# A scan on TensorE whose outputs leave transposed, and the place of its visits between two layers of a gated feed-forward network

## The chip, the core and the metric

The kernel runs on one core of one Trainium2 chip. The metric is the device time of one execution in microseconds (us); the median of three runs is compared. TensorE is called PE below, VectorE DVE, ScalarE ACT, GpSimd POOL and SyncE SP, as in the profile.

## The reference

Two layers, one behind the other. The first is a linear recurrence over 768 steps for 4 sequences of 8 heads with 48 lanes each; its outputs, 3072 rows of 384, go through a gated feed-forward network with 1536 hidden lanes.

```python
state = np.zeros((B, H, D, D))                      # B=4, H=8, D=48
for t in range(S):                                  # S=768
    cur = einsum('bhd,bhe->bhde', u[None] * kt, vt)
    y[:, :, t] = einsum('bhd,bhde->bhe', rt, state + cur)
    state = wt[:, :, :, None] * state + einsum('bhd,bhe->bhde', kt, vt)
...
gate = 1 / (1 + exp(-(x @ w_gate)))                 # x: 3072 x 384, w_gate: 384 x 1536
val = x @ w_val
out = (gate * val) @ w_out
```

## The kernel before

The scan is cut into 24 chunks `q`, each 128 steps of one sequence: `q % 4` is the sequence, `q // 4` the stretch of time. Four chunks of one stretch make a block of 512 rows for the network, `n = q // 4`, so there are six blocks.

For one chunk the two decay scans, `prep_k` (L328) and `prep_r` (L347), run on DVE and scale k and r in place in the tile `pin`; `fade` (L341) scales the old state. PE turns the scaled k (`turn_k`, L361, the tile `pk`) and ACT copies it out. `section1` makes the scores and the sums for the new state (`scores` L374, `sums` L388, the pair of banks `pa`). DVE masks the scores and adds up two states (`settle`). Then the outputs are made (`states` L402 from the stored states, `mix` L417 from masked scores and values, the tile `py`). Here 128 steps lie on the partitions: the scan's outputs have to be turned before the network can use them. So ACT copies them to SBUF (`take_y`, L469), PE turns them (`turn_x`, L472, the tile `px`), ACT takes the rounded part and DVE the remainder (`take_x`, `rest_x`). POOL makes the diagonal (`bonus1` to `bonus4`).

The network works on one of twelve slices `f` of 128 hidden lanes at a time: nine matmuls of `gate` (`pg`, L510), nine of `value` (`pu`, L510), and nine of `down` (`po`, L550), each 128x128 by 512 rows. DVE multiplies gate and value (L528), ACT rounds the product (`hidden_hi`, L532), DVE takes the remainder (`hidden_lo`, L536).

The program is in two stages. In the **first stage** block 0 of the network runs together with chunks 0 to 7 and with the unpacking of the twelve weight slices; a list scheduler (`Plan`) with written costs and ranks (`TURNS`, `COMES`, `LAGS`, `LATE`) fixes the order in which instructions are issued on each engine. In the **main loop** blocks 1 to 5 run in 60 steps `(n, f)`; chunks 8 to 23 are put between. Each step has four slots, and the order on PE is

```python
slot(0); gate(*a); sigmoid(*a)
slot(1); value(*a); hidden(*a); hidden_hi(*a); hidden_lo(*a)
slot(2); down(f - 1)
slot(3)
```

A chunk's outputs and the next chunk's `section1` are issued together, in `both(q)`, which is called the **visit** of q. Slot numbers run on (4 to a step), and what prepares chunk q+1 is put at fixed distances ahead of the visit of q: `prep_k` and `fade` 7 slots before, `turn_k` 5 before, `prep_r` 3 before. A visit stands at slot 7 + 12j of a block in the steady part, that is in slot 3 of a step, behind `down` and ahead of the next `gate`; `FIRST` has the four places of block 1. Engines take their instructions in the order of issue, and wait where an operand is not there. SP issues the loads of later chunks (`load`), and an empty instruction on it (`relay`) hands a bank from one half of PE's rows to the other.

## Time and profile before

| | before |
|---|---|
| median of 3 runs | 586.2 us (586.17 to 589.35) |
| the profiled execution | 585.72 us |
| its span | 583.6 us, granted PE clock 0.996 |
| PE busy | 550.7 us (94%) |
| DVE busy | 325.8 us (56%) |
| ACT busy | 204.6 us (35%) |
| POOL busy | 106.1 us (18%) |

The span reaches from the first to the last instruction of the profiled execution; 2.1 us of its time lie around it. All times within the trace are counted from the start of the span.

### The profile page before, as it was taken

Reading aid. Unit: us, or ns where it says so; the run is one execution under the profiler, and the core shown is the slowest. Engines: PE = TensorE matmul, PEld = TensorE weight load, DVE = VectorE, ACT = ScalarE, POOL = GpSimd, SP = SyncE. Lnnn points to the kernel's source line nnn. Section 1 sums busy time; section 2 is a strip of 40 time slices with the busy share of each in tenths; the row PEclk is TensorE's granted clock in tenths of the full one; section 3 lists DMA queues with packets and bytes.
Section 4 is the critical chain, followed back from the end, with each engine's and each line's share of the span. In section 5 each row is a group of like instructions: output and inputs, shape, how many; then the busy total and the mean of one; then the engine's idle time right before and its main releaser. Section 6 shows DMA issues by size and latency. Waiting matters only on the chain.

```text
span 583.6 us, 13560 instructions
## 1 busy us (share of the span) xinstructions
PE 550.7 (94%) x6044; PEld 460.0 (79%) x6044; DVE 325.8 (56%) x461; ACT 204.6 (35%) x384; POOL 106.1 (18%) x89
## 2 busy tenths in 40 slices
PE   3589999999998999999999999999999999999994
PEld 2468889998777888788888788888788888788883
DVE  4999999976765644554654654654644621221221
ACT  2756596443332323423323323323423322321121
POOL 4540522130211320220210220210220200000000
PEclk9999999999999999999999999999999999999998
DMA  8763925341320222232132231132231100100001
GB/s 269 240 249 91 400 95 171 124 123 50 109 90 11 80 89 56 90 90 57 34 90 55 89 90 54 38 89 59 86 90 47 44 1 2 54 2 0 1 0 60
DMA packets 11046, 50.60 MB, mean 87 GB/s; under 512 B 1265, under 2 KB 1266, under 8 KB 9442
## 3 DMA queue, kind: packets, MB, share of 16 engines
q1 hardware_dynamic: 8818, 45.70, 24.5%
q10 hardware_dynamic: 2160, 3.93, 1.8%
q8 instruction: 49, 0.80, 0.6%
q14 instruction: 19, 0.16, 0.1%
HBM read 44.91 MB, written 4.72 MB: 85 GB/s over the span
## 4 chain that ended last, share of the span: by engine, by line
PE 89%; DVE 5%; DMA 2%; issue 2%; ACT 1%; SPq 0%; DVEq 0%
PE pg L510 24%; PE pu L510 23%; PE po L550 21%; PE py L425 3%; PE py L412 3%; PE pg L507 3%; PE pu L507 3%; PE po L546 3%; PE pa L383 2%; DMA pin<-dec 2%; PE pk L364 2%; PE pa L396 2%; PE px L475 1%; DVE sg L528 1%; DVE hl L536 1%
## 5 line engine op out<-in xcount | busy, mean ns | idle before, releaser
L510 PE MATMUL pg<-x,w 128*128 128x512 f32 (+1 forms) x648 | 153.2, 379 | 0.4 <-ACT sg L521 0.2
L510 PE MATMUL pu<-x,w 128*128 128x512 f32 (+1 forms) x648 | 148.2, 373 | 0.3 <-DVE sg L528 0.3
L528 DVE TENSOR_TENSOR sg<-pu,sg 128x512 f32<-128x512 f32 (+1 forms) x84 | 51.5, 613 | 167.8 <-PE pu L510 162.3
L510 PEld LDWEIGHTS pu<-x,w 128*128 128x128 f32 x648 | 115.2, 188 | 21.9 <-DVE sg L528 0.5
L510 PEld LDWEIGHTS pg<-x,w 128*128 128x128 f32 x648 | 113.3, 188 | 24.2 <-DVE x L495 2.2
L550 PE MATMUL po<-hh,w 128*128 128x512 f32 (+1 forms) x432 | 128.8, 382 | 0.0
L532 ACT CAST hh<-sg 128x512 fp32r<-128x512 f32 (+1 forms) x72 | 42.1, 584 | 129.3 <-DVE sg L528 129.3
L550 PEld LDWEIGHTS po<-hh,w 128*128 128x128 f32 x432 | 77.1, 188 | 12.7
L521 ACT ACTIVATE sg<-pg 128x512 f32<-128x512 f32 (+1 forms) x84 | 44.8, 533 | 111.4 <-PE pg L510 105.4
L550 PE MATMUL po<-hl,w 128*128 128x512 f32 (+1 forms) x216 | 80.6, 373 | 0.7 <-DVE hl L536 0.7
L313 POOL TENSOR_TENSOR bon<-tok,ub 128x384 f32<-128x384 f32 x24 | 34.2, 1424 | 227.7 <-DMA tok<-tok 169.9
L536 DVE TENSOR_TENSOR hl<-sg,hh 128x512 fp32r<-128x512 f32 (+1 forms) x72 | 48.9, 679 | 41.8 <-ACT hh L532 41.7
L326 POOL TENSOR_TENSOR at<-eye,a 128x512 f32<-128x512 f32 x24 | 29.0, 1212 | 129.0 <-DVE a L320 106.1
L550 PEld LDWEIGHTS po<-hl,w 128*128 128x128 f32 x216 | 40.6, 188 | 8.7 <-DVE hl L536 1.2
L316 POOL TENSOR_TENSOR bon<-bon,tok 128x384 f32<-128x384 f32 x24 | 40.1, 1670 | 1.9
L333 DVE TENSOR_TENSOR_SCAN eg<-pin,ends 112x516 f32<-112x516 f32 x24 | 35.4, 1477 | 6.4 <-DMA pin<-dec 5.7
L359 ACT ACTIVATE eg<-eg 112x1032 f32<-112x1032 f32 x24 | 25.6, 1067 | 33.6 <-DVE pin L355 31.7
L412 PE MATMUL py<-mid,pin 48*64 48x48 f32 x384 | 27.0, 228 | 4.4 <-DVE at L452 4.4
L350 DVE TENSOR_TENSOR_SCAN eg<-pin,heads 112x516 f32<-112x516 f32 x24 | 29.9, 1245 | 0.0
L470 ACT COPY bon<-py 128x384 f32<-128x384 f32 x24 | 11.5, 479 | 52.1 <-PE py L425 52.1
L452 DVE COPY_PREDICATED at<-after,pa 128x512 f32<-128x512 int32 x24 | 17.5, 730 | 19.4 <-PE py L412 15.1
L412 PEld LDWEIGHTS py<-mid,pin 48*64 48x64 f32 x384 | 22.4, 140 | 5.4 <-ACT sq L260 4.8
(72 smaller groups left out, 579.6 us busy)
## 6 DMA issues: line engine op xcount, KB each, us to landing
pin<-dec SPq DMA_DIRECT2D x23, 675.5 KB, 5.8
tok<-tok SPq DMA_DIRECT2D x24, 576.0 KB, 6.1
raw<-wts SPq DMA_DIRECT2D x12, 1152.0 KB, 12.1
y<-o ACTq DMA_DIRECT2D x15, 256.0 KB, 2.0
y<-o SPq DMA_DIRECT2D x3, 256.0 KB, 3.3
pin<-dec SPq DMA_DIRECT2D x1, 448.0 KB, 3.9
pin<-dec SPq DMA_DIRECT2D x1, 227.5 KB, 2.8
line<-u SPq DMA_DIRECT2D x1, 1.5 KB
```

The source lines that it names most:

```text
L313: nc.gpsimd.tensor_tensor(out=bon[q], in0=tk[q][:, 0:DM], in1=ub, op=ALU.mult)
L316: nc.gpsimd.tensor_tensor(out=bon[q], in0=bon[q], in1=tk[q][:, DM:2 * DM], op=ALU.mult)
L333: nc.vector.tensor_tensor_scan(out=e[:, 516:0:-1], data0=t[:, 516:0:-1], data1=ends[:, 516:0:-1], initial=0.0, op0=ALU.mult, op1=ALU.add,)
L350: nc.vector.tensor_tensor_scan(out=e[:, WW:WW + 516], data0=t[:, 0:516], data1=heads[:, 0:516], initial=0.0, op0=ALU.mult, op1=ALU.add,)
L412: todo[o].append(lambda p=p, s=s, half=half, o=o, sl=sl: nc.tensor.matmul(spots[o][half, p], lhsT=rr(q)[sl, p, half], rhs=(mid if s else r ...
L507: nc.tensor.matmul(t, lhsT=full(f)[:, cols], rhs=whole[n][:, k, spot], start=k == 0, stop=k == NKT - 1)
L510: nc.tensor.matmul(t, lhsT=w[f][:, cols], rhs=x[n][:, a, k, spot], start=k == 0 and j == 0, stop=k == NKT - 1 and j == 2)
L521: nc.scalar.activation(sg, hid["g", n, f, i0], AF.Sigmoid)
L528: nc.vector.tensor_tensor(out=sg, in0=hid["u", n, f, i0], in1=sg, op=ALU.mult)
L532: nc.scalar.copy(hh, hid["s", n, f, i0])
L536: nc.vector.tensor_tensor(out=hl, in0=hid["s", n, f, i0], in1=hid["hi", n, f, i0].bitcast(F32), op=ALU.subtract)
L550: nc.tensor.matmul(to, lhsT=w[f][:, cols], rhs=h, start=first and i == 0, stop=last and i == 2, skip_group_check=True)
```

## The change

1. In the visit, values and states become the stationary operand, in pieces of 32 lanes, and scores and r become the moving one, 64 steps wide. The outputs then leave with the lanes on the partitions, so `take_y` and `turn_x` go. `scores` and `sums` are cut into stationary pieces of 32 lanes too, so that all matmuls of a visit are in 64x32 tiles.
2. The 48 lanes of a head don't fill whole tiles. Two thirds of the 384 output rows are final; the last third comes in two halves, one in each bank, that have to be added. ACT copies one half (`take_x`), DVE adds the other (`join_x`), ACT rounds it (`last_x`), DVE takes the remainders (`low_x`, `low_last`). The rows of the two upward weights are put in the matching order on the host; values and states get padded places (`tok` grows from 1152 to 1216 columns, the states stand 64 apart in `wide`).
3. The outputs of a visit stand in the bank `turn` and in the bank `pu` that `value` uses. So a visit moves to slot 1, between `gate` and `value`, and at such a step the pending `down` is issued right behind the visit, ahead of `value`.
4. The written costs, ranks and orders of the first stage are new.

```diff
-TURNS = "c0 c1 c2 w0 w1 w2 c3 w3 w4 w5 w6 w7 c4 w8 w9 c5 c6 w10 c7 w11"
+TURNS = "c0 w0 c1 c2 w1 w2 w3 c3 w4 w5 w6 w7 w8 w9 c4 w10 w11 c5 c6 c7"
...
-LAGS = [0, -3.0]
+LAGS = [0, 4.0]
...
-FIRST = [11, 21, 32, 43]
+FIRST = [13, 25, 33, 45]
...
     def scores(q):
...
+                for i in range(half.start, half.stop, 32):
+                    for o in range(2):
+                        sl = slice(64 * o, 64 * o + D)
+                        nc.tensor.matmul(
+                            t[i:i + 32, o, p * HC:(p + 1) * HC], lhsT=kk(q)[sl, p, i:i + 32], rhs=rr(q)[sl, p, half], start=True, stop=True,
+                            skip_group_check=True)
...
+    def states(q):
+        for j in range(2):
             for s, half in enumerate(HALVES):
                 if q < B and not s:
                     continue
+                for p in range(NP):
+                    for o in range(2):
+                        sl = slice(64 * o, 64 * o + D)
+                        i = 64 * p + ((16, 48), (32, 0))[o][j]
+                        nc.tensor.matmul(
+                            lhsT=(mid if s else ready)[q][sl, i:i + 32], rhs=rr(q)[sl, p, half], stop=False, **placed(q, o, p, j, half))
+
+    def mix(q, turn):
+        done = []
+        for j in range(2):
             for p in range(NP):
+                for s, half in enumerate(HALVES):
+                    o = s ^ turn
+                    i = VO + p * L + ((0, 32), (80, 48))[o][j]
+                    done.append(nc.tensor.matmul(
+                        lhsT=tk[q][half, i:i + 32], rhs=att[q][half, o, p], stop=True, **placed(q, o, p, j, half)).ins)
+        return done
...
-    def take_y(q):
-        nc.scalar.copy(bon[q].rearrange("a (p o e) -> a o p e", o=2, e=D), bank["yy", q])
-
-    def turn_x(q):
...
     def both(q):
...
+        bank["y", q] = [att_bank(f"py{q}"), ps1.tile([P, 512], F32, tag="pu", name=f"pz{q}")]
+        states(q)
+        step = relay(mix(q, 0))
+        if q + 1 < NG:
+            section1(q + 1)
+        follow(step, mix(q, 1))
+        take_x(q)
+        join_x(q)
+        last_x(q)
+        low_x(q)
+        low_last(q)
...
-    visit = {q: (q - start) // B * row + (7 + 12 * (q % B) if q >= start + B else FIRST[q - start]) for q in range(start, NG)}
+    visit = {q: (q - start) // B * row + (9 + 12 * (q % B) if q >= start + B else FIRST[q - start]) for q in range(start, NG)}
...
+            visits = ((n - R0) * NFF + f) * 4 + 1 in visit.values()
             slot(1)
+            if visits:
+                down(*last.pop())
             value(*a)
```

How the instructions stand now. In the rows the first number of `pg`, `pu`, `po`, `sg`, `hl` names a group or bank and the second is the slice f; numbers behind the last underscore tell tiles apart.

**PE in block 3, steps 5 to 7, before:** the matmuls around `turn_k` (`pk`) of the next chunk.

```order
L550 MATMUL po_2_3791<-hl_0_4_4020,w_723 128x512
L510 MATMUL pg_0_6_4174<-x_2997,w_1076 128x512 x9
L510 MATMUL pu_0_6_4186<-x_2997,w_1076 128x512 x9
L364 MATMUL pk_4201<-ident,pin_4119 128x112 x4
L550 MATMUL po_0_3789<-hh_0_5_4146,w_869 128x512 x2
L550 MATMUL po_0_3789<-hl_0_5_4148,w_869 128x512
```

**The same place with the change:**

```order
L545 MATMUL pg_0_6_5017<-x_3581,w_1283 128x512 x9
L545 MATMUL pu_0_6_5029<-x_3581,w_1283 128x512 x9
L585 MATMUL po_0_4544<-hh_0_5_5013,w_1041 128x512 x2
L585 MATMUL po_0_4544<-hl_0_5_5015,w_1041 128x512
L585 MATMUL po_1_4545<-hh_0_5_5013,w_1041 128x512 x2
L585 MATMUL po_1_4545<-hl_0_5_5015,w_1041 128x512
L585 MATMUL po_2_4546<-hh_0_5_5013,w_1041 128x512 x2
L585 MATMUL po_2_4546<-hl_0_5_5015,w_1041 128x512
L373 MATMUL pk_5061<-ident,pin_4989 128x112 x4
L545 MATMUL pg_0_7_5068<-x_3581,w_1356 128x512 x9
```

`turn_k` stood behind `value` and ahead of `down`; it now stands behind both, ahead of the next `gate`.

**DVE at the same place, before:** `prep_k` (the scan into `eg`, the reciprocal, the product into `pin`), `fade`, and the products of the network around them.

```order
L528 TENSOR_TENSOR sg_0_5_4133<-pu_0_5_4135,sg_0_5_4133 128x512
L536 TENSOR_TENSOR hl_0_5_4148<-sg_0_5_4133,hh_0_5_4146 128x512
L495 TENSOR_TENSOR x_3924<-px_4150,x_3924 128x3x128
L333 SCALAR_TENSOR_TENSOR eg_4168<-pin_4119,ends 112x516
L337 RECIPROCAL heads<-eg_4168 112x4
L339 TENSOR_TENSOR pin_4119<-pin_4119,eg_4168 112x512
L345 TENSOR_TENSOR ready_4172<-state_104,eg_4168 112x192
L528 TENSOR_TENSOR sg_0_6_4184<-pu_0_6_4186,sg_0_6_4184 128x512
```

**With the change:**

```order
L571 TENSOR_TENSOR hl_0_5_5015<-sg_0_5_4844,hh_0_5_5013 128x512
L563 TENSOR_TENSOR sg_0_6_5027<-pu_0_6_5029,sg_0_6_5027 128x512
L571 TENSOR_TENSOR hl_0_6_5042<-sg_0_6_5027,hh_0_6_5040 128x512
L339 SCALAR_TENSOR_TENSOR eg_5047<-pin_4989,ends 112x516
L343 RECIPROCAL heads<-eg_5047 112x4
L345 TENSOR_TENSOR pin_4989<-pin_4989,eg_5047 112x512
L354 TENSOR_TENSOR wide_105<-state_103,eg_5047 112x4x48
L563 TENSOR_TENSOR sg_0_7_5078<-pu_0_7_5080,sg_0_7_5078 128x512
```

The scan stood ahead of the two products of step 6; it now stands behind both of them.

**PE in block 1 with the change, step 6,** where the visit of chunk 9 has taken its `down` with it and chunk 11 is prepared (before, a `down` stood between `value` and this `pk`):

```order
L585 MATMUL po_2_2294<-hl_0_5_2614,w_1041 128x512
L545 MATMUL pu_0_6_2800<-x_1298,w_1283 128x512 x9
L373 MATMUL pk_2823<-ident,pin_2787 128x112 x4
L545 MATMUL pg_0_7_2830<-x_1298,w_1356 128x512 x9
L545 MATMUL pu_0_7_2842<-x_1298,w_1356 128x512 x9
```

`turn_k` stands right behind `value` there, with no matmul between.

## The prediction

> **What bounds the kernel now.** First the page: totals, then busy tenths in 40 slices of 14.6 us (9 is 90% or more). Then a table by stretches: length, busy time of PE, weight loads, DVE, ACT, POOL, granted clock, DMA share.

> ```profile
> span 583.6 us, 13560 instructions
> ...
> PE   3589999999998999999999999999999999999994
> ...
> DVE  4999999976765644554654654654644621221221
> ...
> 60.00:90.00 30.00, 28.88 (x344) 26.79 (x343) 29.27 (x40) 20.85 (x39) 11.45 (x6) 1.00 0.56 231
> 145.90:208.37 62.47, 58.96 (x774) 48.04 (x773) 38.29 (x58) 19.64 (x37) 13.98 (x10) 1.00 0.22 68
> 208.37:295.90 87.53, 87.48 (x993) 71.90 (x993) 45.86 (x70) 26.17 (x51) 15.76 (x12) 1.00 0.23 69
> ```

> The first stage (to 146 us) fills DVE and PE alike: 29.27 and 28.88 of 30 us. In the main loop PE has 87.48 of 87.53 us and DVE half: whatever PE does or waits for there counts in full, and DVE counts only where PE waits for it. The chain of waits shows one cycle of three steps (start, us, what):

> ```profile
> 274.10 2.28 PE pg L510 x9
> 276.38 2.06 PE pu L510 x9
> 278.43 0.33 PE px L475 x3
> 278.76 2.09 PE po L550 x9
> ...
> 291.52 2.04 PE po L550 x9
> ```

> Nine matmuls take 2.04 us undisturbed; the transposes `px` take 0.33 and lengthen what follows by 0.05. The visit itself, in order of time (start, us):

> ```profile
> 293.17 0.39 PE L550 MATMUL po<-hl,w 128*128 128x512 f32 x1
> 293.49 0.25 PE L412 MATMUL py<-ready,pin 48*64 48x48 f32 x1
> ...
> 293.58 0.22 PE L412 MATMUL py<-ready,pin 48*64 48x48 f32 x1
> ...
> 293.64 0.22 PE L412 MATMUL py<-ready,pin 48*64 48x48 f32 x1
> ...
> 295.02 0.88 PE L425 MATMUL py<-tok,at 64*32 64x48 f32 x64
> 295.83 0.96 PE L510 MATMUL pg<-x,w 128*128 128x512 f32 x3
> ```

> It lasts from 293.49 to 295.83, 2.34 us. A tile of PE starts a new matmul every 0.06 us in the 64x64 part (293.58, 293.64); in the 64x32 part 64 of them start within 0.88 - 0.2 = 0.68 us on four tiles, 0.042 us each.

> **Part 1, the transposes go.** 16 visits in the main loop x (0.33 + 0.05) = **-6.1 us**. ACT's copy `take_y` lies beside matmuls and gives nothing.

> **Part 2, the visit in 64x32 tiles.** Each fp32 matmul is recorded twice. Now there are 4 x 32 matmuls, 256 records, evenly over eight tiles: 32 on each, 24 with 64 moving columns and 8 with 48. At 0.058 us and 0.042 us that is 24 x 0.058 + 8 x 0.042 = 1.73 us, with 0.13 to leave the mode (0.81 us from 295.02 to 295.83, less 0.68) 1.86 us, **-0.5 us a visit, -8 for 16**. The trace shows only four tiles busy at a time, so eight is the unknown. Upper end: four at a time, 48 x 0.058 + 16 x 0.042 + 0.13 = 3.6 us, +1.25 a visit. Lower end: every record at 0.042, 1.5 us, -0.85. I take eight, because sharing is already the rule in the row: four 64x32 tiles each keep their own 0.042 us. [...]

> [...]

> **Part 3, the visit moves; what was behind and ahead of it.** `value` waits until the bank `pu` is read out, by a copy and two activations on ACT and a remainder on DVE. Groups (busy, mean ns):

> ```profile
> L495 DVE TENSOR_TENSOR x<-px,x 128x384 fp32r<-128x384 f32 x22 | 12.1, 552 | 4.9 <-ACT x L490 4.9
> L470 ACT COPY bon<-py 128x384 f32<-128x384 f32 x24 | 11.5, 479 | 52.1 <-PE py L425 52.1
> L467 DVE TENSOR_TENSOR state<-pa,mid 112x192 f32<-112x192 f32 x20 | 7.1, 353 | 0.4
> L490 ACT ACTIVATION_READ_ACCUMULATOR x<-px 128x1 f32 x22 | 4.2, 193 | 0.0
> ```

> At 128 columns a DVE operation is 353 - 64 x (552 - 353)/192 = 0.29 us, an ACT one below 0.35. Three on ACT, two reads of 0.19 and one on DVE make at most 1.7 us; the `down` now ahead of `value` is 2.04. Cover holds: **0**; were it gone, up to 1.7 a visit. The wider `tok` (1216 columns for 1152) lands 5% later, long before its visit: 0.

> But the fixed distances move too. `prep_k` was issued in slot 0 and `turn_k` in slot 2, with `gate` and `value` (4.1 us) between; now they fall in slot 2 of one step and slot 0 of the next, with one `down` (2.04 us) between, and on DVE the scan stands behind both products of the step, which wait for `value`. The trace of before has one such place: chunk 9's visit stood in slot 21, a slot 1, and its `turn_k` had the same neighbours.

> ```profile
> 169.63 2.22 PE L510 MATMUL pu<-x,w 128*128 128x512 f32 x9
> ...
> 171.96 0.69 DVE L528 TENSOR_TENSOR sg<-pu,sg 128x512 f32<-128x512 f32 x1 [2.35 <-PE pu L510]
> ...
> 172.68 0.62 ACT L532 CAST hh<-sg 128x512 fp32r<-128x512 f32 x1 [2.19 <-DVE sg L528]
> ...
> 173.34 0.69 DVE L536 TENSOR_TENSOR hl<-sg,hh 128x512 fp32r<-128x512 f32 x1 [0.69 <-ACT hh L532]
> ...
> 173.51 1.38 POOL L313 TENSOR_TENSOR bon<-tok,ub 128x384 f32<-128x384 f32 x1 [7.42 <-DMA tok<-tok]
> ...
> 173.88 0.39 PE L550 MATMUL po<-hl,w 128*128 128x512 f32 x1
> 173.94 0.55 DVE L495 TENSOR_TENSOR x<-px,x 128x384 fp32r<-128x384 f32 x1
> 174.41 1.56 DVE L333 TENSOR_TENSOR_SCAN eg<-pin,ends 112x516 f32<-112x516 f32 x1
> 174.96 1.80 POOL L316 TENSOR_TENSOR bon<-bon,tok 128x384 f32<-128x384 f32 x1
> 176.01 0.18 DVE L337 RECIPROCAL heads<-eg 112x4 f32<-112x4 f32 x1
> 176.10 1.21 DVE L339 TENSOR_TENSOR pin<-pin,eg 112x512 f32<-112x512 f32 x1
> ...
> 177.41 0.57 PE L364 MATMUL pk<-ident,pin 112*128 112x112 f32 x4 [3.15 <-issue]
> ```

> PE stands idle for 3.15 us: the scaled k that `pk` reads is finished at 177.31. That it is not so in the steady part of before, and how fast DVE is without POOL beside it, show the rows of the later cycle:

> ```profile
> 282.74 2.21 PE L510 MATMUL pu<-x,w 128*128 128x512 f32 x9
> ...
> 283.55 0.66 DVE L339 TENSOR_TENSOR pin<-pin,eg 112x512 f32<-112x512 f32 x1
> ...
> 284.79 0.55 PE L364 MATMUL pk<-ident,pin 112*128 112x112 f32 x4
> ...
> 287.05 1.23 DVE L350 TENSOR_TENSOR_SCAN eg<-pin,heads 112x516 f32<-112x516 f32 x1
> ```

> There the product ends at 284.21, ahead of the end of `value`. With the change, from the start of L528 on: 2.07 us to the end of L536 (171.96 to 174.03), 1.23 for the scan, 0.13 to the product's start (176.10 less 174.41 less 1.56), 0.66, and 0.10 to `pk` (177.41 less 177.31): 4.19. L528 starts 0.11 after `value` ends (169.63 + 2.22 = 171.85), so PE has finished `down` at 2.04 - 0.11 = 1.93. **The stall is 4.19 - 1.93 = 2.26 us.** Behind `pk` on PE stands the next `gate`, and nothing passes it: the stall counts in full. The values without POOL hold if POOL is done:

> ```profile
> 167.62 0.35 SPq L300 DMA_DIRECT2D tok<-tok  x1
> ```

> POOL started (173.51) 5.9 us after this issue of its load, which follows a visit's end, and its two operations took 1.38 + 1.80 at the stall: done some 9 us after the visit, while the scan starts at 2.1 + 3 x 2.04 + 0.1 + 2.07 = 10.4. This happens for chunks 10 and 12 to 23: 13 x 2.26 = **+29.4**. With POOL beside it, each would be 2.07 + 1.56 + 0.13 + 1.21 + 0.10 - 1.93 = 3.14, the upper end.

> For chunk 11 the visit of chunk 9 has taken `down` away, and `pk` follows `value` at once; the scan starts 2.1 + 2.05 + 0.1 + 2.07 = 6.3 us after that visit, when POOL works: 5.07 + 0.11 = **+5.2**. The stall of 3.15 at chunk 10's `pk` in before is already within the 29.4: **-3.15**.

> **Part 4, the first stage.** Per chunk DVE gets 0.29 + 0.42 + 0.29 for 0.55 us (chunks 0 and 1: 0.29 for nothing): +3.3 in all; PE saves 8 x (0.38 + 0.3), at most 5.5. Both engines are nearly full and the order is new, so ends are -5 and +6; nearest to the DVE row: **+1**.

> **Sum**, against the profiled execution's 585.7 (median of the runs 586.2): -6.1 - 8 + 29.4 + 5.2 - 3.15 + 1 = +18.3: **604 us**.

> [...] Here 3.15 idle us left the clock at 1.00 in the stretch 145.90:208.37. [...]

> **The rivals.** (a) Only four tiles run at once: 16 x (1.25 + 0.5) = 28 more, **632**. For it: no row shows more than four; against: they didn't slow each other. (b) POOL is beside every scan: 13 x (3.14 - 2.26) = 11.4 more, **615**. For it: L339 took 1.21 at the stall; against: POOL's timing above. (c) The other side: `pk` doesn't wait, because DVE has the scan done within `down`. It decides at 1.93 us from L528's start; then 604 - 29.4 - 5.2 = **569.5**. For it: the steady cycle of before has no such stall; against: the scan stands behind products that alone take 2.07. (d) That `pk` is no longer at that place, or the tiles don't run as written: the issue order shows both, no weight.

> **How the numbers follow.** Forecast 0.63, (a) 0.14, (b) 0.15, (c) 0.08. The forecast's own spread: stalls between 1.9 and 2.6 (5 us either way), the first stage (5), the visit (0.35 x 16 = 6 below): 593 to 614. With (b) the range is 592 to 622, which leaves out most of (a) and (c). One per cent (5.9 us) is about what a measurement of this kernel tells from no change. Slower 0.90, same 0.04 (short stalls, fast visits), faster 0.06.

> **What would show it.** Right: idle before `pk` of 2.0 to 2.5 us 13 times, released by DVE's product, and one near 5; a block of 87.5 us becomes 87.5 + 4 x (2.26 - 0.88) = 93; no `px`; visits near 1.9 us; no idle before `pu`. Wrong: visits above 2.3 us (tiles), scans of 1.5 us (POOL), a main loop that starts more than 6 us from 146, or no idle before `pk`.

## The result, and the profile after

The changed kernel takes 674.7 us (median of four runs, 668.5 to 678.2) against 586.2 before: a ratio of 1.148, 95% interval 1.140 to 1.157. Slower was right; the forecast of 604, and its range to 622, were not. The profiled execution took 678.2 us, with a span of 676.4, so 92.8 more than the span before. The page after: its span, PE's busy tenths and granted clock (slices of 16.9 us), and one row of the DMA queues (packets, MB, share):

```profile
span 676.4 us, 17932 instructions
...
PE   4577899989887788879888788878888889999993
...
PEclk9979999989999899999899989989789999999997
...
q8 instruction: 66, 1.08, 0.7%
```

In the main loop PE is mostly under 90%, up to the last seven slices, and its clock dips along the whole span. The last row counts transfers of instructions: 66 of 16 KB. Before there were 49:

```profile
q8 instruction: 49, 0.80, 0.6%
```

By stretches (columns as in the prediction's table), a block of four visits and a piece of the first stage:

```profile
275.15:384.59 109.44, 93.21 (x1364) 74.44 (x1364) 44.74 (x82) 27.39 (x67) 13.19 (x12) 0.97 0.19 57
60.00:90.00 30.00, 25.24 (x231) 22.02 (x230) 26.73 (x31) 20.13 (x37) 9.72 (x7) 0.94 0.56 222
```

The block took 87.53 us before and should have taken 93; it takes 109.44, and PE lacks 16 us in it. In the first stage PE is down from 28.88 to 25.24 of 30 us and DVE from 29.27 to 26.73. The chain of waits shows one cycle of it (start, us, what):

```profile
244.10 2.10 PE pu L545 x9
246.21 2.09 PE po L585 x9
248.30 2.12 issue
250.42 0.57 PE pk L373 x4
250.99 2.11 PE pg L545 x9
...
260.46 0.61 PE pa L391 x34
261.12 0.42 PE pa L402 x30
261.54 2.21 issue
263.74 0.31 PE pa L402 x12
...
264.45 2.29 PE po L585 x9
...
301.62 2.12 issue
303.74 0.57 PE pk L373 x4
304.31 3.66 PE pg L545 x9
```

Four things stand here. Ahead of `pk` PE is idle for 2.12 us, the stall that was forecast. In the middle of the visit (259.41 to 264.45) it is idle for 2.21 us, between two matmuls of the same line, which is in no term of the prediction. Nine large matmuls take 2.10 us, not 2.04. And after the stall at 301.62 nine take 3.66: the granted clock is 0.50 from 304.26 to 307.67, for 3.41 us. The waits from 160 to 592 us (engine and what waited, in total, times, longest):

```profile
PE pk L373 <- issue: 32.1, 14, 4.6
...
PE pa L402 <- issue: 19.5, 10, 2.3
...
PE pz L433 <- issue: 4.0, 2, 2.1
...
PE py L433 <- issue: 2.2, 1, 2.2
...
PEld pz L433 <- SPq L439: 0.3, 1, 0.3
```

Fourteen stalls ahead of `pk`, and thirteen (10 + 2 + 1) inside visits, 25.7 us in all. The bank relay over SP, the suspect at such a place, costs 0.3 us once. What comes in during the stall at 261.5 is shown by the DMA queues between 261.33 and 262.40 us (packets, MB, share):

```profile
q8 instruction: 1, 0.02, 5.4%
```

One 16 KB packet of instructions starts at 261.39 us and takes 0.93; PE goes on 1.4 us after its end. It is so in all thirteen: the packet starts 0.1 to 0.9 us before the stall, and PE goes on 1.3 to 1.6 us after its end. And counted from the start of the program, the stalls come behind matmul records number 2890, 3274, 3529, 3913, 4296, 4552, 4935, 5319, 5574, 5958, 6341, 6597 and 7236: the distances are 384, 255, 384, 383, 256 and so on, multiples of 128 to within one. A packet holds the instructions of 128 records (a weight load and a multiplication each): the 8148 records of PE would fill 64 packets, the 6044 of before 47, close to the 66 and 49 counted. A visit of 256 records would use up two packets in some 2.6 us, and the second isn't there yet. Four of the last visits have 224 records; two of these don't stall, and by this count the boundaries there stand after 109 records alone and after 2 and 130.

### The profile page after: what moved, and what is told of

Read it like the earlier page. It is cut to its first block, busy times and chain, and to the rows that moved or that the text cites. A ratio compares the mean times of both kernels' runs of the same rounds, so it can differ in the third digit from the quotient of the medians.

```text
span 676.4 us, 17932 instructions
## 1 busy us (share of the span) xinstructions
PE 575.1 (85%) x8148; PEld 468.1 (69%) x8148; DVE 323.2 (48%) x524; ACT 208.8 (31%) x464; POOL 93.9 (14%) x92
## 4 chain that ended last, share of the span: by engine, by line
PE 75%; issue 11%; DVE 9%; ACT 2%; DMA 1%; POOL 1%; SPq 0%; DVEq 0%; POOLq 0%; ACTq 0%
PE po L585 20%; PE pg L545 20%; PE pu L545 19%; PE pa L391 2%; PE pg L542 2%; PE pa L402 2%; PE py L423 2%; PE pk L373 2%; PE py L433 2%; PE pu L542 1%; DVE eg L339 1%; PE po L581 1%; DMA tok<-tok 1%; DVE temp L273 1%; DVE w L287 1%
## 5 line engine op out<-in xcount | busy, mean ns | idle before, releaser
L545 PE MATMUL pg<-x,w 128*128 128x512 f32 (+1 forms) x648 | 160.3, 394 | 1.1 <-ACT sg L556 1.0
L545 PEld LDWEIGHTS pg<-x,w 128*128 128x128 f32 x648 | 119.5, 197 | 26.5 <-ACT sg L556 1.8
L319 POOL TENSOR_TENSOR bon<-tok,ub 128x384 f32<-128x384 f32 x24 | 29.3, 1220 | 194.9 <-DMA tok<-tok 125.9
L373 PE MATMUL pk<-ident,pin 112*128 112x112 f32 x96 | 16.4, 301 | 39.7 <-issue 32.1
L514 DVE TENSOR_TENSOR bon<-py,bon 128x128 f32<-128x128 f32 x24 | 7.0, 291 | 82.7 <-ACT x L511 77.4
L373 PEld LDWEIGHTS pk<-ident,pin 112*128 112x128 f32 x96 | 11.1, 158 | 48.3 <-issue 42.7
L402 PE MATMUL pa<-tok,kT 64*32 64x48 f32 (+1 forms) x1408 | 21.9, 218 | 21.4 <-issue 21.1
L402 PEld LDWEIGHTS pa<-tok,kT 64*32 64x32 f32 (+1 forms) x1408 | 16.9, 105 | 23.2 <-issue 23.1
L433 PE MATMUL py<-at,tok 64*32 64x64 f32 x1024 | 28.8, 238 | 4.8 <-issue 4.1
L339 DVE TENSOR_TENSOR_SCAN eg<-pin,ends 112x516 f32<-112x516 f32 x24 | 30.5, 1270 | 4.5 <-DMA pin<-dec 3.7
```

Source lines behind the costliest of these rows:

```text
L319: nc.gpsimd.tensor_tensor(out=bon[q], in0=tk[q][:, 0:DM], in1=ub, op=ALU.mult)
L339: nc.vector.tensor_tensor_scan(out=e[:, 516:0:-1], data0=t[:, 516:0:-1], data1=ends[:, 516:0:-1], initial=0.0, op0=ALU.mult, op1=ALU.add,)
L373: nc.tensor.transpose(out=t[:, p * L:(p + 1) * L], in_=kk(q)[:, p], identity=ident[:L, :L])
L402: nc.tensor.matmul(t[i:i + m, s, NP * HC + p * D:NP * HC + (p + 1) * D], lhsT=kT[q][half, p * L + i:p * L + i + m], rhs=values(q, p, i // ...
L433: done.append(nc.tensor.matmul(lhsT=tk[q][half, i:i + 32], rhs=att[q][half, o, p], stop=True, **placed(q, o, p, j, half)).ins)
L545: nc.tensor.matmul(t, lhsT=w[f][:, cols], rhs=x[n][:, a, k, spot], start=k == 0 and j == 0, stop=k == NKT - 1 and j == 2)
```

## The experiments

**The early scan.** The cause of the stall ahead of `pk`, tried by its own edit:

```
-                prepare(q + 1, time - 7, time - 5, time - 3)
+                free = visit.get(q - 1, 0)
+                prepare(q + 1, time - 9 if time - 9 > free else time - 7, time - 5, time - 3)
```

> The changed kernel with the scan of the next chunk (bonus1, bonus2, prep_k, fade) issued nine slots ahead of a visit instead of seven (chunk 11 alone keeps seven); nothing else moves, and TensorE's own order stays as it is. Theory: pk waits for DVE's scan and product, which stand behind the step's two products. Then the thirteen gaps of 2.27 us ahead of pk go (29.5 us), and with them some of the eight half-clock windows in the main loop that follow them (1.7 us each): 674.7 becomes 635 to 647. Rival 1: pk waits for its bank (the readers of py on ACT and DVE): the gaps stay and the time stays within 5 us of 675. Rival 2: DVE is late again because the scan now meets POOL or the load of its pin: gaps of 0.5 to 1.5 us remain, 650 to 665. The stalls inside the visits should stay under all three.

645.5 us, ratio 1.100 (1.096 to 1.105; all ratios are against the kernel before, run beside it). In the chain `pk` now follows `po` at once, and takes 0.39 us instead of 0.57:

```profile
246.22 2.10 PE po L585 x9
248.31 0.39 PE pk L373 x4
248.70 2.12 PE pg L545 x9
```

All thirteen gaps are gone, that of chunk 11 (4.7 us) stays, and the stalls in the visits stay. The 29.2 us gained are the 13 x 2.27 from one start to the next; of the half-clock windows of 3.41 us seven remain of eight, so they come behind the other stalls as well. The mechanism and the size of the prediction's largest term are shown.

**Fewer records in a visit.** Scores and sums back in 64x64 tiles:

```
-                for i in range(half.start, half.stop, 32):
...
-                            t[i:i + 32, o, p * HC:(p + 1) * HC], lhsT=kk(q)[sl, p, i:i + 32], ...
+                        t[half, o, p * HC:(p + 1) * HC], lhsT=kk(q)[sl, p, half], ...
...
-            for i, m in ((0, 32), (64, 32), (32, 32), (96, 16)):
+            for i, m in ((0, 64), (64, D)):
```

> The changed kernel with scores and sums in 64x64 tiles as before (16 + 16 matmuls instead of 32 + 32): a visit then has 192 matmul records instead of 256. Theory: a visit stalls because TensorE's instructions come in packets of 16 KB, one for every 128 matmul records, and 256 records in 2.6 us use up two of them faster than one can be fetched. With 192 records the stalls of 1.6 to 2.3 us become shorter by the time of the slower pace or fall away in some visits: 0 to 1.3 us each, and still only on the grid of 128 records; about 12 to 30 us less, 645 to 663. Rival 1: the stall belongs to the bank relay over SP, which stays as it is: 14 stalls of 1.6 to 2.3 us, each beside the relay's matmuls, time within 6 us of 675. Rival 2: sums waits for the copy of kT: unchanged too, all stalls at the first matmuls of sums.

647.1 us, ratio 1.104 (1.100 to 1.109). Nine of the fifteen visits with scores have no stall and take 2.55 us; six have one of 0.8 to 1.2 us, now in `mix` instead of `sums`:

```profile
265.00 0.62 PE pa L390 x32
265.62 0.44 PE pa L401 x26
266.06 0.17 PE pz L432
...
266.42 1.16 issue
267.58 0.21 PE pz L432
```

They too stand on the grid of 128 records, and which visits have one follows from it: those in which the first packet boundary comes after more than some 20 of the visit's records and the second still falls into it. With 256 records two always do, with 192 in about half of the cases. The first stage is cured as well: the main loop's first large matmul starts at 144.4 us, 159.0 in the changed kernel. Both rivals (relay, copy of kT) fall: neither was touched.

**More records in the kernel before.** Each score matmul four times:

```
-        theirs, more = (scores(q + 1), sums(q + 1)) if some else ([], [])
+        theirs, more = (scores(q + 1) * 4, sums(q + 1)) if some else ([], [])
```

> The kernel before with each of the 16 score matmuls of a visit issued four times (the same values written again): 128 matmuls and 256 records a visit as in the change, but in the old tiles, the old order and with the old addresses. Theory of the instruction packets: a gap of 1 to 2.3 us appears in most of the 15 visits that carry scores, on a grid of 128 records, beside some 0.8 us a visit for 96 more records: 586 becomes 608 to 630. Rival (the stall belongs to the eight tiles, the new order or the relay's new place): only the 0.8 us, 15 x 0.8 = 12, so 595 to 600, no gap.

632.3 us, ratio 1.080 (1.076 to 1.084): above both ranges, and not for the reason tested. A visit of 256 records takes 5.1 us instead of 2.35, 20 ns a record. The list takes the scores of one row of tiles at a time, which by the author's reading of the code leaves them two tiles; no run tried it. At that pace PE was idle for only 0.2 to 0.7 us, in five visits, on the grid again:

```profile
339.06 0.38 PE py L425 x22
339.44 0.31 issue
339.75 0.69 PE py L425 x42
```

As a test it is weak: it shows that the pace matters beside the number.

**The same records, further apart.** On top of the early scan, the next chunk's scores are issued three slots ahead of the visit:

```
+                    prepare(q + 1, time - 9, time - 5, time - 5)
+                    at(time - 3, weights, q + 1)
```

> The changed kernel with the early scan of the run e1_early, and the score matmuls of the next chunk taken out of the visit and issued three slots ahead of it (its r scan five slots ahead): the same 256 records in the same 64x32 tiles, but in two bursts of 64 and 192 with 18 large matmuls (4.2 us) between. Theory of the instruction packets: what counts is how many records fall into the time of one fetch, so the stalls of 1.9 to 2.7 us of e1_early fall to 0 to 1.2 us, a few visits only: 645.5 becomes 618 to 632. Rival 1 (the stall comes with the tiles' number or the relay): 14 stalls of about 2 us stay, 643 to 648. Rival 2 (the total of instructions counts, fetching is the bottleneck on average): they move to other places, 640 to 648.

629.5 us, ratio 1.072 (1.067 to 1.077). Of the nine visits that now have 192 records five run through in 1.99 us and four stall for 1.9 to 2.5 us; the four of 160 records don't stall, and two that keep all 256 (those that score chunks 9 and 11) do. Tiles, relay and the total of instructions are the same as in the run with the early scan alone, so the burst decides, and rivals 1 and 2 fall. The stalls that are left aren't shorter, against the expectation; they come in fewer visits.

**Addresses.** The change had moved the weights to 192 bytes beyond a multiple of 256, and x, sg, hh and hl to 128 beyond one. First the weights alone are moved back (`sides` is a tile of 64 bytes ahead of them, in which the two `a0` now live):

```
+    sides = const.tile([P, 2 * H], F32, name="sides")
...
-        bank["a0", q] = p2.tile([P, H], F32, tag="a0", name=f"a0{q}")
+        bank["a0", q] = sides[:, q % 2 * H:(q % 2 + 1) * H]
```

> The changed kernel with one tile of 64 bytes a partition put ahead of the weights (it takes in the two small tiles a0, so that everything behind them lies where it was): the weights lie at a multiple of 256 bytes again, as in the kernel before, where the change had them at 192 beyond one. Theory: TensorE reads or loads weights at that offset more slowly, and nine 512-column matmuls that take 2.10 us come back to 2.04: 1620 matmuls x 0.0062 us = 10 us less, 665 (with the spread of this kernel's runs 659 to 670). Rival 1: it is the moving side (x, sg, hh at 128 beyond a multiple of 256), and 2.10 stays. Rival 2: it is the power or clock state, and 2.10 stays. Stalls in the visits and ahead of pk stay under all three.

676.8 us, ratio 1.153 (1.148 to 1.157): nothing. From start to start large matmuls take 232.8 ns on the mean, 233.3 in the changed kernel, 228.1 before. Then the moving side alone, in both directions:

```
+    p1.tile([P, 32], F32, name="margin")        # changed kernel; "shift" in the kernel before
...
-        sq = stage.tile([P, 3 * DM], F32, tag="sq", name=f"sq{f}")
+        sq = stage.tile([P, 3 * DM], BF16, tag="sq", name=f"sq{f}")     # changed kernel only
```

> The changed kernel with 128 bytes a partition put ahead of its scan tiles, so that the moving side of the feed-forward matmuls (x, sg, hh, hl) lies at multiples of 256 bytes again; the weights stay at 192 beyond one. (The scratch of the guard on the weights becomes bf16, to make room.) Theory: the moving side at 128 beyond a multiple of 256 costs each 512-column matmul 6 ns: 233.3 ns from start to start becomes 227 to 228.5, and 674.7 becomes 664 to 668. Rival: neither address matters (moving the weights alone gave 232.8 instead of 233.3 and no time), and the rhythm comes with the change itself (the permuted rows, the denser instruction stream): 233 stays, 670 to 679.

> The kernel before with 128 bytes a partition put ahead of its scan tiles: x, sg, hh and hl then lie at 128 beyond a multiple of 256 as in the change, the weights stay at a multiple of 256, nothing else moves. Theory of the moving side: 227 to 228 ns from start to start becomes 232 to 234, 586.3 becomes 593 to 597. Rival (addresses don't matter): 585 to 588 and 228 ns.

In the changed kernel 233.3 ns become 229.1; one line of its chain, then two of the kernel before with the shift, where 228.1 ns became 232.7:

```profile
245.29 2.06 PE pu L547 x9
```

```profile
222.99 2.10 PE po L552 x9
225.09 2.09 PE pg L512 x9
```

The kernel before went to 594.3 us, ratio 1.013 (1.010 to 1.016): 1620 x 4.6 ns = 7.5 us, the whole difference of 7.5. So the address of the moving operand costs what was seen, with nothing else changed. The changed kernel stayed at 674.0 us, though: its matmuls gained 6.8 us, and its profiled execution has 13 half-clock windows in the main loop instead of 8, each 1.7 us, so the gain was lost to the clock. The expectation of 664 to 668 left that out, and why the windows are more no run shows.

**What limits a record.** On top of the run with the scores apart, `mix` takes half of its columns:

```
+                    n = HC // 2 if q >= (R0 + 1) * B else HC
-                        lhsT=tk[q][half, i:i + 32], rhs=att[q][half, o, p], ...
+                        lhsT=tk[q][half, i:i + 32], rhs=att[q][half, o, p, :n], ...
```

> The kernel of e6_apart, where the mix matmuls of the main loop's chunks take only the first 32 of their 64 moving columns, so half of that sum is left out of the output; as many matmuls and records as there. In e6_apart the 64 records of mix start 7.7 to 10 ns apart, and the 60 of states, which keep their 64 columns, 9.75 ns. If each tile is busy with its columns (the prediction's term: 58 ns for 64 columns on eight tiles, 7.3 ns), mix comes down to 4 to 5 ns a record, and a visit without a stall from 1.99 to 1.75 to 1.85 us. If TensorE can't start records of small tiles faster than about one in 8 ns, whatever their columns, mix stays at 7.5 to 10 ns and the visit at 1.95 to 2.0 us. The total is 620 to 632 in both.

The first and the last of the 32 records of `mix`'s second half in one visit, with 64 columns and then with 32:

```profile
306.23 0.24 PE L433 MATMUL pz<-at,tok 64*32 64x64 f32 x1
...
306.58 0.22 PE L433 MATMUL py<-at,tok 64*32 64x64 f32 x1
```

```profile
307.40 0.21 PE L434 MATMUL pz<-at,tok 64*32 64x32 f32 x1
...
307.72 0.19 PE L434 MATMUL py<-at,tok 64*32 64x32 f32 x1
```

(306.58 - 306.23) / 31 = 11.3 ns from start to start with all columns, (307.72 - 307.40) / 31 = 10.3 with half of them. Three records of `sums` start in between; counted with them it is 10.2 and 9.4. The visit goes from 1.99 to 1.92 us, and the one run took 629.7. The matmuls start one after another at about this pace with 32 columns as with 64, though each lasts 0.2 us and they overlap on eight tiles. Whether the weight loads or the issue set the pace was not tried. (The 7.7 ns of the expectation came from a few visits; over the same stretch it is 11 to 12.)

**All of it together.** Early scan, 64x64 tiles in `section1`, scores apart, `turn_k` of chunk 11 two slots later, both addresses:

> The changed kernel with all that the theories name: early scan (e1_early), scores and sums in 64x64 tiles (e3_tiles64), scores three slots ahead of the visit, the transposes of chunk 11 two slots later, and weights and moving side at multiples of 256 bytes. If the stalls ahead of pk, the instruction stalls and the addresses make up the loss: a main loop of 426 to 436 us after a first stage of 144 to 147, no gap over 1 us ahead of pk or in a visit, 573 to 586. Rival (something else in the change costs time, as half-clock windows without a stall before them or the larger readout on ACT and DVE): 590 to 610, and the gaps show where.

590.8 us, ratio 1.008 (1.005 to 1.011). In the main loop the large matmuls start from 146.5 to 578.2 us, 431.7 us as expected (426 to 436), but the first stage is 0.8 us longer than before, 10.1 us instead of 7.8 follow the start of the last large matmul, and two visits still stall, for 1.41 and 1.20 us. Two small shifts next:

```
-                    prepare(q + 1, time - 9, time - 5, time - 5)
+                    prepare(q + 1, time - 9, time - 3, time - 5)
...
-                prepare(q + 1, 5, 7, 8)
+                prepare(q + 1, 5, 7, 9)
```

> The kernel of e8_all with two shifts of issue slots: the transposes pk stand right ahead of the scores, three slots before the visit (one excursion of TensorE into small tiles less, some 0.3 us x 13 = 4), and the guard of chunk 9 is issued behind the sigmoid of its step instead of ahead of it (a gap of 1.28 us at 165 us goes). Theory that each excursion costs at its edges: 590.8 becomes 584 to 588, the same as before within 1 per cent. Rival (edges belong to each change of tile shape, so joining gains nothing, or pk now waits for something): 588 to 592. In both the instruction stalls may move, since the grid of 128 records shifts by nothing but their surroundings do: 0 to 3 visits with 1 to 1.7 us.

590.2 us, ratio 1.0045 (1.002 to 1.007). Joining `pk` with the scores gained 0.06 us from visit to visit, so the theory of the edges falls; the gap at 165 us went; and the two stalls stayed. Then the sharpest test of the grid: one matmul five times more, once, before the main loop's visits.

```
+        if q == (R0 + 1) * B:
+            for _ in range(5):
+                nc.tensor.matmul(
+                    bank["a", q][:HC, 0, :HC], lhsT=kk(q)[:D, 0, :HC], rhs=rr(q)[:D, 0, :HC], ...
```

> The kernel of e9_joined with one score matmul issued five times more, once, ahead of chunk 8's scores: ten matmul records (0.15 us) that move every later visit by ten against the grid of 128 records. Theory: a visit stalls when the first packet boundary in it comes after more than some 20 of its records and a second one still falls in it. In e9_joined that holds for the two visits with boundaries after 24 and 152, and 26 and 154 records (gaps of 2.05 and 1.56 us); ten later they stand at 14 and 142, and 16 and 144, where visits of other runs did not stall, and no other visit comes into the range. So no visit stalls, the half-clock window at 255 us goes too, the main loop is 426 to 428 us instead of 431.7, and 590.2 becomes 585 to 587. Rival (the stalls depend on time, such as what other traffic the packets meet): one or two stalls stay or move to other visits, 589 to 592.

586.2 us, ratio 0.999 (0.997 to 1.001). The same visit, without and with the ten records more:

```profile
251.70 0.60 PE pa L404 x26
252.30 0.17 PE pz L435
...
252.66 1.84 issue
254.49 0.21 PE pz L435
```

```profile
250.70 0.60 PE pa L404 x26
251.30 0.17 PE pz L435
...
251.68 2.26 PE po L596 x9
```

No visit stalls, no clock is halved in the main loop, which takes 427.7 us. One idle time of 0.74 us is left at 362.11, three matmuls behind the end of a visit, at a boundary of packets again: the rule of the visit's own records is not the whole of it. Adding work that is used for nothing made the kernel 4 us faster. This is the best version of the change, and no faster than the kernel before.

**The grid in the kernel before.** The same five matmuls, in the kernel before:

```
-        go(scores(q) + sums(q))
+        some = scores(q)
+        go(some[:1] * (5 if q == (R0 + 1) * B else 0) + some + sums(q))
```

> The kernel before with one score matmul issued five times more ahead of chunk 8's scores, so that its later visits move by ten records against the grid. Before, the boundaries of chunk 8's visit stand after 36 to 39 records (one only, no stall). Theory: with ten more they stand after 26 to 29 and 154 to 157 of its 160 records, and this visit alone gets a gap of 0.8 to 1.4 us near its end (3.0 to 3.2 us from boundary to boundary, less the 1.85 us that 128 records take there); the other 14 visits stay at 2.35 us. Rival: no gap in any visit. The total is 585 to 590 in both.

Chunk 8's visit, and no other, got a gap:

```profile
165.23 0.18 PE py L412
...
166.76 0.80 PE py L425 x60
167.56 1.09 issue
168.65 0.28 PE py L425 x4
```

The kernel before was not free of the limit; its visits lay well on it. From visit to visit it has 248 records, 8 less than two packets, so the boundary moves by only 8, and none of its visits had two boundaries in the bad range. One run gave 589.8 us: beside the gap of 1.09 the clock was halved for 6.8 us at the idle 3.12 us ahead of chunk 10's `pk`, where 3.15 us before had left it at 1.00.

## Why the prediction was right or wrong

**Part 1, the transposes:** gone as forecast; the -6.1 us was not tried by itself.

**Part 2, the visit, -8 us:** the failed step. It has two errors. The term itself: 58 ns for a tile's record, shared by eight tiles, made 7.3 ns a record. No row of before shows eight tiles at once. In the visits with the scores apart `mix` runs on eight, and its records overlap: each lasts 0.22 to 0.24 us. But they start some 10 ns apart (10.2, and 9.4 with half the columns), so 256 records would take some 2.6 us without a stall where 1.86 was forecast and 160 took 2.35 before. The prediction's own row had it: 64 records in 0.68 us on four tiles are 10.8 ns apart, nearly the pace on eight. What it read as each tile's own 0.042 us was the pace of all records together. And a term that was missing: the supply of instructions. All visits together take 31.7 us more than before instead of 8 less, 25.7 of it idle. The row that could have told it was on the page of before, 49 packets of 16 KB (shown above) for 6044 records, 123 each; the visit's 256 records stand in the working. "The trace shows only four tiles busy at a time, so eight is the unknown" looked for the unknown in the array, not ahead of it. With half the columns the pace changed by about 1 ns in 10, where the expectation by that term was 4 to 5 ns a record.

**Part 3, the moved steps:** right. Thirteen stalls of 2.12 us ahead of `pk` (2.27 from start to start beyond the usual) for 2.26, one of 4.60 for 5.2, by the chain that was worked out:

```profile
246.31 0.69 DVE L563 TENSOR_TENSOR sg<-pu,sg 128x512 f32<-128x512 f32 x1 [2.20 <-PE pu L545]
...
248.30 1.23 DVE L339 TENSOR_TENSOR_SCAN eg<-pin,ends 112x516 f32<-112x516 f32 x1
...
249.65 0.66 DVE L345 TENSOR_TENSOR pin<-pin,eg 112x512 f32<-112x512 f32 x1
...
250.42 0.57 PE L373 MATMUL pk<-ident,pin 112*128 112x112 f32 x4 [2.12 <-issue]
```

The scan takes 1.23, so POOL is not beside it (rival b), and taking the stalls away gave 29.2 us for 29.4. The cover of `pz` held, and the relay cost 0.3 us once.

**Part 4, the first stage, +1 us:** wrong by 12.3. The main loop starts at 159.0 instead of 145.7, and with 64x64 tiles in `section1` alone at 144.4. Of the 14.6 us between these two, 5.5 are three stalls during which a packet lands (behind records 349, 983 and 1999), and 5.1 the clock, halved for 13.7 us there and for 3.4 with 64x64 tiles; the rest was not traced.

**Not in the sum at all:** the addresses, 1620 x 5.2 ns = 8.4 us, and the clock. The trace has eight windows of 3.41 us at half clock in the main loop, 8 x 1.7 = 13.7 us; seven start between 0.4 us ahead of and 0.6 us behind the end of a stall of 1.86 to 4.6 us, and one follows another window. The prediction had as evidence only the 3.15 us of before that left the clock at 1.00; but at the same place 3.13 us cost one window in the kernel before with its moving operands shifted, and 3.12 us two in the last run. One instance was not enough to leave the clock out.

The excess adds up: visits 39.7 (31.7 + 8), first stage 12.3, clock 13.7, addresses 8.4, together 74.1 us, where 74.5 lie between the forecast's 18.3 and the 92.8 of the spans. It fits that well partly by luck: the end of the program, 10.6 us behind the start of the last large matmul instead of 7.8, is in none of these terms, so they overlap by some 2 us.

**The rivals:** (a), four tiles, 632, was the nearest, but not what happened. (b) and (c) fell with the stalls of Part 3. None named a limit ahead of the array, so the range couldn't hold the time.

## What to carry to other kernels

Count instructions as well as columns: the small matmuls of these visits started some 10 ns apart with 32 columns as with 64, and where a visit of 224 or 256 records came to a second packet boundary before that packet had landed, PE stood still for 1.6 to 2.3 us. When a program's length shifts, or a small tile is added or dropped, check where the bursts fall on the packet grid and where the moving operands lie before a gain or a loss is put down to the change itself: here ten records more went with 4 us less, and 128 bytes cost 7.5 us. A step moved by a fixed number of slots moves past other engines' queues: that part could be worked out to 0.15 us from the rows of before.
